# Retention attention and a gelu MLP on one core: quarter-array transposes and values in chunks 1 to 5, masked score blocks left out and k, v loaded with swapped token halves in chunks 2 to 5

## The chip, the cores and the metric

The kernel runs on one core of a Trainium2 chip. The core has TensorE (PE in the profile; its weight loads are PEld), VectorE (DVE), ScalarE (ACT), GpSimd (POOL) and SyncE (SP, which here only issues transfers). Each takes its instructions in order from its own queue. The metric is the device time of one execution in microseconds (us); lower is better.

## The reference

A retention recurrence with a decay per head gives `attn_out`; a two-layer MLP with a tanh gelu follows. Batch 4, 8 heads, 768 tokens, head size 64; d_model 512, d_ff 2048.

```python
def _attn_ref(q, k, v):
    gamma = 1.0 - 2.0 ** (-5.0 - np.arange(H, dtype=np.float32))
    scale = 1.0 / np.sqrt(D)
    ...
    for t in range(S):
        state = gamma[None, :, None, None] * state + np.einsum('bhd,bhe->bhde', k[:, :, t], v[:, :, t])
        y[:, :, t] = scale * np.einsum('bhd,bhde->bhe', q[:, :, t], state)
...
def _moe_ref(x, w_in, w_out):
    h = x @ w_in
    ...
    g = 0.5 * h * (1.0 + np.tanh(c * (h + 0.044715 * h * h * h)))
    return (g @ w_out).astype(np.float32)
```

## The kernel before

**Tiling.** The 768 tokens are cut into 6 chunks of 128 (c = 0 to 5). Inside a chunk the recurrence is turned into matrix products: transposes of q and k (`mm_T`, L266), scores of every key token against every query token (`mm_A`, L273), a causal mask with the decay laid over them on the way out of PSUM (`ev_A1`, L328), the part of the output that comes from the state carried over (`mm_yc`, L289), the part from the chunk's own values (`mm_yi`, L306), and the update of the state (`mm_s` and `ev_S2`). The scores' eviction writes f16 tiles `a` that the values step uses as moving operand. The MLP of a chunk then runs as seven products per block, with sums of weights and activations made by DVE and POOL (L432): `m1w_mm` (L530) for the first layer, `m2w_mm` (L542) for the second; chunk 0 and part of chunk 1 run it plainly (L407, L553).

**TensorE's use of its array.** The MLP products and the transposes use all 128 rows and 128 columns. A transpose by `mm_T` takes a pair of heads, 128x128, so a batch has 8 of them (q and k, 4 pairs each), or 4 in chunks 3 to 5 (`BLK`), where q is transposed by DVE (`trq`, L689). Scores and `mm_yc` use quarters, 64 rows by 64 columns; four of them (two heads j, two halves m of the key tokens) follow one another into the four quarters. A score quarter has 128 columns, all query tokens of the chunk, also where the block of 64 queries by 64 keys lies wholly above the diagonal. `mm_yi` and `mm_s` use all 128 rows and 64 columns.

**Evictions.** `evT` and `evTk` copy transposes from PSUM to SBUF in one instruction per batch (1024 columns, or 512 in chunks 3 to 5); `evA` is one DVE instruction of 512 columns per batch and head parity j; `evY` one per batch.

**Loads.** `load_in` (L765) issues one transfer of 256 KB per input, chunk and batch on SP's queue, all 8 heads, tokens on the partitions. `q_load` (L704) issues 16 of 64 KB for a chunk of `BLK`. `load_dec` (L697) brings a table for `ev_Y1`. Loads and stores keep one order on SP. The weights are triggered from POOL (`trig`, L751), and `hold` (L755) keeps the loads of chunk 1 behind the last trigger and a gelu of chunk 0.

**Order.** Every step is registered as an item with the engines that may run it, and the list `ORDER` (L16) names all items in one sequence, with the letter of the engine for each: p TensorE, a ACT, v DVE, g POOL, s SP (w stands for spin matmuls). Each engine runs its own items in that order and waits in line for what an item needs. PSUM banks (8) and SBUF slots are given out in the same sequence.

## Time and profile before

| | us |
|---|---|
| median of 3 runs | 203.11 (201.61 to 208.5) |
| profiled execution | 201.71 |
| its span, first to last instruction | 199.9 |
| attention steps on PE, busy time over all chunks: L269 128x128 transposes / L278 scores / L309 values / L297 from the state | 10.1 + 1.3 / 7.4 + 0.8 / 6.9 + 1.3 / 3.7 |
| MLP steps on PE, busy time, L542 / L530 / L407 | 69.1 / 63.0 / 31.6 |
| DVE: L329 score evictions, 44 of 512 columns | 27.3 (682 ns each) |
| DVE / ACT: L219 / L217 copies of transposes, 1024 columns | 679 ns / 1017 ns |
| DVE / ACT: the same, 512 columns | 410 ns / 584 ns |
| DVE: L432 `o` with 512 columns / with 256 | 682 ns / 420 ns |
| ACT: one-column activation, L184 | 203 ns |

The page lists, for an engine and a line, how many instructions there are and their busy time; the timeline lists runs of like instructions with their start and length in us. Matmuls overlap, so the length of a run on PE reaches past the start of the next run; what it occupied is the distance between the two starts. The granted TensorE clock is 1.00 in every stage.

### The profile page before, as it was taken

How to read it: one execution, taken by the hardware profiler on the slowest of the kernel's cores; microseconds unless marked ns; L12 is line 12 of the kernel's file. 1: busy time of each engine (PE TensorE's matmuls, PEld its weight loads, DVE VectorE, ACT ScalarE, POOL GpSimd, SP SyncE). 2: the span in 40 equal slices, each digit the busy share in tenths (PEclk: the TensorE clock that was granted, in tenths of full speed). 3: DMA queues.
4: the chain of work that ended last, by engine and by line, in shares of the span. 5: the costliest groups of instructions: out<-in, count | busy, mean ns of one | idle time of the engine just before them, and what ended most of it. 6: DMA issues, size and time to landing. Idle time of an engine off the chain costs nothing.

```text
span 199.9 us, 5916 instructions
## 1 busy us (share of the span) xinstructions
PE 192.4 (96%) x2460; PEld 157.5 (79%) x2460; DVE 151.7 (76%) x278; ACT 123.0 (62%) x233; POOL 108.7 (54%) x109
## 2 busy tenths in 40 slices
PE   7999999989999999999999999999999999999993
PEld 2447895555889898789888899888988888888882
DVE  4366008599788999999999898899697879948730
ACT  2466474023578609999863889857779636786411
POOL 0657000021218575997899579898704967269500
PEclk9999999999999999999999999999999999999999
DMA  6999999998999779987996797610000500002204
GB/s 159 284 267 207 207 204 196 219 258 184 230 241 252 135 132 242 268 130 130 274 257 122 123 223 190 192 48 0 3 0 0 213 3 0 3 0 107 108 26 184
DMA packets 95898, 30.11 MB, mean 151 GB/s; under 512 B 88320, under 2 KB 92800, under 8 KB 95872
## 3 DMA queue, kind: packets, MB, share of 16 engines
q1 hardware_dynamic: 85120, 23.45, 50.6%
q0 software_dynamic: 4224, 4.19, 12.6%
q10 hardware_dynamic: 6528, 2.10, 4.2%
q8 instruction: 19, 0.31, 0.6%
q14 instruction: 7, 0.06, 0.1%
HBM read 27.64 MB, written 6.29 MB: 170 GB/s over the span
## 4 chain that ended last, share of the span: by engine, by line
PE 61%; DMA 14%; DVE 9%; SPq 7%; ACT 3%; POOL 2%; issue 1%; DVEq 0%; ACTq 0%
PE ps L542 26%; PE ps L530 20%; DMA w_out<-in_moe_w_out_dram 10%; PE ps L407 5%; SPq L713 4%; DMA ld<-in_v_dram 3%; SPq L164 3%; PE ps L269 2%; PE ps L278 2%; PE ps L309 2%; PE ps L553 2%; ACT qk L217 2%; DMA ldq<-in_q_dram 1%; DVE s_g L432 1%; DVE st L432 1%
## 5 line engine op out<-in xcount | busy, mean ns | idle before, releaser
L423 ACT ACTIVATE g<-ps 128x512 f16<-128x512 f32 (+1 forms) x56 | 28.3, 538 | 20.6 <-PE ps L407 16.8
L432 DVE TENSOR_TENSOR st<-ps,st 128x512 f32<-128x512 f32 x48 | 31.4, 680 | 5.9 <-PE ps L530 3.0
L542 PEld LDWEIGHTS <-s_g 128*128 128x128 f16 x320 | 31.1, 98 | 4.0 <-DVE s_g L432 0.4
L432 POOL TENSOR_TENSOR s_g<-g 128x512 f16<-128x512 f16 x21 | 24.7, 1184 | 16.9 <-ACT g L423 9.4
L423 ACT ACTIVATE g<-st 128x512 f16<-128x512 f32 x48 | 28.6, 629 | 8.2 <-DVE st L432 7.9
L217 ACT COPY st<-ps 128x512 f32<-128x512 f32 x48 | 26.5, 593 | 8.9 <-PE ps L530 8.8
L407 PE MATMUL ps<-x,w_in 128*128 128x256 f16 (+1 forms) x320 | 30.3, 251 | 0.1
L329 DVE TENSOR_TENSOR a<-ps,mask 128x512 f16<-128x512 f32 x44 | 27.3, 682 | 3.6 <-PE ps L278 3.5
L407 PEld LDWEIGHTS <-w_in 128*128 128x128 f16 x320 | 25.6, 98 | 3.4 <-DMA w_in<-in_moe_w_in_dram 0.3
L530 PEld LDWEIGHTS <-w_in 128*128 128x128 f16 x256 | 24.8, 98 | 3.3 <-issue 0.4
L542 PEld LDWEIGHTS <-g 128*128 128x128 f16 x240 | 22.9, 98 | 3.2
L217 ACT COPY o<-ps 128x512 f32<-128x512 f32 (+1 forms) x28 | 14.5, 528 | 13.8 <-PE ps L542 9.5
L530 PEld LDWEIGHTS <-u_w 128*128 128x128 f16 x192 | 18.5, 98 | 3.2 <-ACT st L217 0.7
L542 PE MATMUL ps<-w_out,s_g 128*128 128x256 f16 x160 | 19.9, 273 | 0.1
L542 PE MATMUL ps<-t_w,s_g 128*128 128x256 f16 x160 | 19.6, 273 | 0.0
L542 PE MATMUL ps<-w_out,g 128*128 128x256 f16 x160 | 19.5, 273 | 0.0
L530 PE MATMUL ps<-xs,u_w 128*128 128x256 f16 x128 | 17.8, 272 | 0.7 <-ACT st L217 0.4
L432 POOL TENSOR_TENSOR s_g<-s_g,g 128x512 f16<-128x512 f16 x14 | 16.3, 1169 | 3.8 <-DVE s_g L432 3.2
L530 PE MATMUL ps<-xs,w_in 128*128 128x256 f16 x128 | 18.4, 273 | 0.0
L432 POOL TENSOR_TENSOR s_g<-g,s_g 128x512 f16<-128x512 f16 x15 | 17.4, 1169 | 1.0 <-DVE s_g L432 0.8
L530 PE MATMUL ps<-x,w_in 128*128 128x256 f16 x128 | 17.4, 273 | 0.2 <-DVE st L432 0.2
L432 DVE TENSOR_TENSOR s_g<-g 128x512 f16<-128x512 f16 x19 | 15.2, 815 | 2.4 <-ACT g L423 2.1
(68 smaller groups left out, 289.7 us busy)
## 6 DMA issues: line engine op xcount, KB each, us to landing
ld<-in_v_dram SPq DMA_DIRECT2D x19, 256.0 KB, 4.3
ld<-in_k_dram SPq DMA_DIRECT2D x17, 256.0 KB, 4.4
out_dram<-o SPq DMA_DIRECT2D x8, 512.0 KB, 3.2
ldq<-in_q_dram SPq DMA_DIRECT2D x48, 64.0 KB, 2.7
w_in<-in_moe_w_in_dram POOLq DMA_DIRECT2D x4, 512.0 KB, 10.3
w_out<-in_moe_w_out_dram POOLq DMA_DIRECT2D x4, 512.0 KB, 15.1
ld<-in_q_dram SPq DMA_DIRECT2D x5, 256.0 KB, 4.5
out_dram<-o SPq DMA_DIRECT2D x5, 256.0 KB, 3.8
```

The costliest lines, as they stand in the source:

```text
L164: eng.dma_start(out=raw[nm, c, b], in_=srcs[nm][b, :, c * C:(c + 1) * C, :].rearrange("h p d -> p h d"),)
L217: eng.copy(out=out, in_=in_)
L269: nc.tensor.transpose(out=ps[:, i, hp], in_=pair(h16[nm, c, b], hp), identity=iden)
L278: nc.tensor.matmul(out=ps[j][m * 64:(m + 1) * 64, hp], lhsT=t[j * 64:(j + 1) * 64, 1, hp, m * 64:(m + 1) * 64], rhs=t[j * 64:(j + 1) * 64, ...
L309: nc.tensor.matmul(out=ps[j * 64:(j + 1) * 64, hp], lhsT=h16["v", c, b][:, 2 * hp + j], rhs=a_sb[c, b, j][:, hp], start=(c == 0), stop=Tru ...
L329: eng.tensor_tensor(out=a_sb[c, b, j], in0=ps, in1=mask[:, j], op=ALU.mult)
L407: nc.tensor.matmul(out=out, lhsT=w_in_sb[wi][:, kc, wr * 128:(wr + 1) * 128], rhs=xT[c][:, kc, t0:t1], start=(kc == 0), stop=(kc == NHP - ...
L423: nc.scalar.activation(out=out, in_=in_, func=AF.Gelu_apprx_tanh, scale=1.0)
L432: eng.tensor_tensor(out=out, in0=in0, in1=in1, op=op)
L530: nc.tensor.matmul(out=ps[:, f], lhsT=m1_lhs(lk, kc, 2 * g + f), rhs=x[:, kc], start=(n in FIRST and kc == 0 and f == 0), stop=(n in (1, 5 ...
L542: nc.tensor.matmul(out=ps, lhsT=m2_lhs(c, lk, fp, a), rhs=m2_rhs(rk, fp), start=(first and fp == 0), stop=(n in (1, 5, 6) and fp == NP - 1 ...
L713: eng.dma_start(out=t[p0:p0 + 32, :, a, :], in_=src[j, dd, t0:t0 + 32])
```

## The change

- Chunks 1 to 5: transposes are made by `mm_T2`, 64x64 at a time, four quarters of the array in turn, and land in two PSUM banks, one for each half m of the tokens. Two copies of half the size (`evTk`, `evTh`) bring them to SBUF.
- Chunks 2 to 5 (`SW` = 2): k and v of heads 4 to 7 are loaded with the two halves of the chunk's tokens swapped on the partitions. `load_in` issues three transfers for it: heads 0 to 3 whole (128 KB), and 64 KB for each half of heads 4 to 7. The new table `cs2` (106 KB, loaded with `dec`) holds k's decay for the swapped order and what the new mask is made of.
- Chunks 2 to 5: scores leave out the block of late keys against early queries, which the mask zeroed. Per pair of heads, one half of the partitions has 128 columns and the other 64; `halves` gives which. `evA2` evicts 384 columns instead of 512. The mask for it is written by two instructions (`scam`) over the old one, after chunk 1's score evictions.
- Chunks 1 to 5: values are made by `mm_yi2` for a pair of batches in two turns of 16 quarter products; in each turn the two row halves write different batches. Between the turns stands `peek`, a copy of one element that needs the first turn's result, and the second turn needs `peek`.
- `ORDER` is new throughout. TensorE's quarter work of chunk 3 reads before: T b2, T b1, T b0, T b3 (in four places); A b2, b3, b0; A b1, yc, yc, S, yi b2, b0, b3, S, yi b1. After (a semicolon stands for MLP work in between): T b0, b1; T b2, b3; A b1, b2, b0; A b3, yc, yc, first turn (0,1); second turn (0,1), first turn (2,3), S, S, second turn (2,3).

The diff, with the lists of `ORDER` left out:

```diff
--- before.py
+++ after.py
@@ -14,58 +14,60 @@
 ORDER = """
...
 """
@@ -102,6 +104,16 @@
     gst_o = np.where(p_i[:, None] < 64, g128[None, 1::2], g128[None, 0::2])
+    late = (p_i[:, None] + 64.0) % 128.0
+    vdec = np.concatenate([kdec[:, :4], gam[None, 4:] ** (160.0 - late)], axis=1)
+    hp_long = np.where(p_i < 64, 0, 2)[:, None, None] + np.arange(2)[None, None, :]
+    ig = np.stack(
+        [1.0 / g128[2 * hp + np.arange(2)[None, :, None]] for hp in (hp_long, (hp_long + 2) % 4)],
+        axis=-1,
+    ).reshape(128, 8)
+    sees = (p_i[:, None] % 64 <= p_i[None, :]).astype(np.float64)
+    cs2_np = np.concatenate([vdec, ig, sees, sees[:, :64]], axis=1).astype(np.float32)
+    cs2_h = nc.inline_tensor(cs2_np, name="rr_cs2")
@@ -120,6 +132,7 @@
     cst = const.tile([128, 192], F32)
+    cs2 = const.tile([128, 16 + 192], F32)
@@ -142,6 +155,7 @@
     BLK = (3, 4, 5)
+    SW = 2
@@ -230,11 +244,11 @@
         else:
-            col = OQ if nm == "q" else OK
+            tab = cst[:, OQ:OQ + H] if nm == "q" else (cs2 if c >= SW else cst[:, OK:])[:, 0:H]
...
                 in0=heads(src, sw),
-                in1=heads(cst[:, col:col + H].unsqueeze(2), sw).broadcast_to(
+                in1=heads(tab.unsqueeze(2), sw).broadcast_to(
@@ -270,15 +284,38 @@
 
+    def mm_T2(c, b, ps, nms):
+        for i, nm in enumerate(nms):
+            for hp in range(NHP):
+                for m in range(2):
+                    rows = slice(m * 64, (m + 1) * 64)
+                    for j in range(2):
+                        nc.tensor.transpose(
+                            out=ps[m][j * 64:(j + 1) * 64, i, hp],
+                            in_=h16[nm, c, b][rows, 2 * hp + j],
+                            identity=iden[rows, rows],
+                        )
...
+    def halves(c, hp):
...
+        if c < SW:
+            return (0, 0, slice(0, 128), hp), (1, 64, slice(64, 128), hp)
+        far = hp > 1
+        return (far, 0, slice(0, 128), hp % 2), (1 - far, 64, slice(128, 192), hp % 2)
...
+    HPS = (0, 2, 1, 3)
...
         t = qkT[c, b]
-        for hp in range(NHP):
-            for m in range(2):
+        for hp in HPS:
+            for m, t0, cols, x in halves(c, hp):
+                if c < SW:
+                    t0, cols = 0, slice(0, 128)
...
                     nc.tensor.matmul(
-                        out=ps[j][m * 64:(m + 1) * 64, hp],
+                        out=ps[j][m * 64:(m + 1) * 64, x, cols],
                         lhsT=t[j * 64:(j + 1) * 64, 1, hp, m * 64:(m + 1) * 64],
-                        rhs=t[j * 64:(j + 1) * 64, 0, hp],
+                        rhs=t[j * 64:(j + 1) * 64, 0, hp, t0:],
@@ -325,8 +362,37 @@
 
+    def mm_yi2(c, bs, ps, turn):
+        for hp in HPS if turn == 0 else HPS[::-1]:
+            for m, t0, cols, x in halves(c, hp):
+                for j in (0, 1) if turn == 0 else (1, 0):
+                    b = bs[m ^ j ^ turn]
+                    nc.tensor.matmul(
+                        out=ps[b][j * 64:(j + 1) * 64, hp, t0:],
+                        lhsT=h16["v", c, b][m * 64:(m + 1) * 64, 2 * hp + j],
+                        rhs=a_sb[c, b, j][m * 64:(m + 1) * 64, x, cols],
+                        start=False,
+                        stop=(turn == 1),
+                        skip_group_check=True,
+                    )
...
+    mask2 = mask.rearrange("p j hp t -> p (j hp t)")[:, 0:768].rearrange(
+        "p (j x t) -> p j x t", j=2, x=2
+    )
...
+    def new_mask(eng, n):
+        lo, hi = ((0, 128), (128, 192))[n]
+        shape = [128, 2, 2, hi - lo]
+        eng.tensor_tensor(
+            out=mask2[:, :, :, lo:hi],
+            in0=cs2[:, 16 + lo:16 + hi].unsqueeze(1).unsqueeze(1).broadcast_to(shape),
+            in1=cs2[:, 8 + n:16:2].rearrange("p (j x) -> p j x", j=2).unsqueeze(3).broadcast_to(shape),
+            op=ALU.mult,
+        )
...
     def ev_A1(eng, c, b, j, ps):
-        eng.tensor_tensor(out=a_sb[c, b, j], in0=ps, in1=mask[:, j], op=ALU.mult)
+        m = mask2 if c >= SW else mask
+        eng.tensor_tensor(out=a_sb[c, b, j], in0=ps, in1=m[:, j], op=ALU.mult)
@@ -603,7 +669,10 @@
         add="v",
+        peek="va",
         evA="v",
+        evA2="v",
+        scam="vg",
@@ -617,6 +686,7 @@
         evTk="va",
+        evTh="va",
@@ -626,6 +696,7 @@
         sume="gv",
+        load3="s",
@@ -697,6 +768,7 @@
             eng.dma_start(out=dec.rearrange("p h t -> p (h t)"), in_=dec_h.ap())
+            eng.dma_start(out=cs2, in_=cs2_h.ap())
@@ -766,13 +838,28 @@
 
+        swap = c >= SW and nm != "q"
...
         def emit(eng):
-            eng.dma_start(
-                out=T[ldk], in_=srcs[nm][b, :, c * C:(c + 1) * C, :].rearrange("h p d -> p h d")
-            )
+            if not swap:
+                eng.dma_start(
+                    out=T[ldk], in_=srcs[nm][b, :, c * C:(c + 1) * C, :].rearrange("h p d -> p h d")
+                )
+                return
+            lo, hi, t0 = slice(0, 64), slice(64, 128), c * C
+            for rows, hs, at in (
+                (slice(0, 128), slice(0, 4), t0),
+                (lo, slice(4, 8), t0 + 64),
+                (hi, slice(4, 8), t0),
+            ):
+                n = rows.stop - rows.start
+                eng.dma_start(
+                    out=T[ldk][rows, hs],
+                    in_=srcs[nm][b, hs, at:at + n, :].rearrange("h p d -> p h d"),
+                )
...
         shape = (SIZE["ld"][1],) if ldk[0] == "st" else ()
-        op("load", emit, [prev[0]], [key], alloc=[(ldk, 1, *shape)],
+        op("load3" if swap else "load", emit, [prev[0]], [key], alloc=[(ldk, 1, *shape)],
@@ -788,22 +875,36 @@
 
+        def T2(b):
+            nms = "k" if c in BLK else "qk"
...
+            def emit():
+                mm_T2(c, b, [T["bank", "T", c, b, m] for m in range(2)], nms)
...
+            for m in range(2):
+                def ev(eng, m=m):
+                    qkT[c, b] = T["qkT", c, b]
+                    copy_on(
+                        eng,
+                        qkT[c, b][:, 2 - len(nms):, :, m * 64:(m + 1) * 64],
+                        T["bank", "T", c, b, m],
+                    )
...
+                new = c not in BLK and m == 0
+                op("evTk" if len(nms) > 1 else "evTh", ev,
+                   [("T", c, b)] + ([] if new else [("al", "qkT", c, b)]), [("kT", c, b, m)],
+                   alloc=[(("qkT", c, b), 1)] if new else [],
+                   early=[("al", "qkT", c, b)] if new else [], free=[("bank", "T", c, b, m)])
+            pe(0.235 if len(nms) > 1 else 0.13, emit, [(nm + "16", c, b) for nm in nms],
+               [("T", c, b)],
+               [(("bank", "T", c, b, m), 1, (128, len(nms), NHP, 64), F16) for m in range(2)],
+               [("qk16", c, b)])
...
         def T1(b):
+            if c:
+                return T2(b)
...
-            if c in BLK:
-                def emit():
-                    mm_T(c, b, T["bank", "T", c, b], "k")
...
-                def ev(eng):
-                    copy_on(eng, T["qkT", c, b][:, 1], T["bank", "T", c, b][:, 0])
...
-                op("evTk", ev, [("T", c, b), ("al", "qkT", c, b)], [("kT", c, b)],
-                   free=[("bank", "T", c, b)])
-                return pe(0.24, emit, [("k16", c, b)], [("T", c, b)],
-                            [(("bank", "T", c, b), 1, (128, 1, NHP, 128), F16)],
-                            [("qk16", c, b)])
@@ -826,11 +927,16 @@
 
-                op("evA", ev, [("A", c, b)], [("a", c, b, j)], alloc=[(("a", c, b, j), 1)],
+                new = c >= SW
+                shape = ((128, 2, 192),) if new else ()
+                op("evA2" if new else "evA", ev, [("A", c, b)] + (["mask0", "mask1"] if new else []), [("a", c, b, j)],
+                   alloc=[(("a", c, b, j), 1, *shape)],
                    free=[("bank", "A", c, b, r)])
-            got = [("qT", c, b), ("kT", c, b)] if c in BLK else [("qkT", c, b)]
+            got = [("kT", c, b, m) for m in range(2)] if c else [("qkT", c, b)]
+            if c in BLK:
+                got.append(("qT", c, b))
             pe(cost, emit, got, [("A", c, b)],
-                       [(("bank", "A", c, b, j), 1) for j in range(2)], [] if c else [("qkT", c, b)])
+                       [(("bank", "A", c, b, j), 1, *(((128, 2, 192),) if c >= SW else ())) for j in range(2)], [] if c else [("qkT", c, b)])
@@ -853,8 +959,26 @@
                early=[] if has_x else [("al", "x", c)], free=[("bank", "Y", c, b)])
+            if c:
+                return
...
+        def yi2(bs):
+            def emit(turn):
+                mm_yi2(c, bs, {b: T["bank", "Y", c, b] for b in bs}, turn)
...
+            def peek(eng):
+                b = bs[halves(c, HPS[-1])[1][0] ^ 1]
+                copy_on(eng, misc[64:65, 1:2], T["bank", "Y", c, b][64:65, HPS[-1], C - 1:C])
...
+            a_of = [("a", c, b, j) for b in bs for j in range(2)]
+            did = ("Yh", c, bs[0])
+            pe(0.182, lambda: emit(0), a_of + [("v16", c, b) for b in bs]
+                       + [("Yc", c, b) for b in bs], [did])
+            op("peek", peek, [did], [("peek", c, bs[0])])
+            pe(0.182, lambda: emit(1), [("peek", c, bs[0])], [("Y", c, b) for b in bs], [],
+                       a_of + [("v16", c, b) for b in bs])
@@ -882,6 +1006,8 @@
                 S1(b)
+        for bs in ((0, 1), (2, 3)) if c else ():
+            yi2(bs)
@@ -1213,6 +1339,10 @@
 
+    for n in range(2):
+        op("scam", lambda eng, n=n: new_mask(eng, n),
+           ["dec"] + [("a", SW - 1, b, j) for b in range(B) if SW > 1 or b > 1 for j in range(2)],
+           [f"mask{n}"])
...
     for c in range(1, NCk):
```

## The prediction

> **What bounds the kernel now.** I read the page's engine table first, then its 40 slices, then the table by stage, the chain of waits, and the timeline of single engines where TensorE changes its work.
>
> ```profile
> PE 192.4 (96%) x2460; PEld 157.5 (79%) x2460; DVE 151.7 (76%) x278; ACT 123.0 (62%) x233; POOL 108.7 (54%) x109
> PE   7999999989999999999999999999999999999993
> DMA  6999999998999779987996797610000500002204
> ```
>
> TensorE (PE) is the only engine that is busy from the second slice to the last but one; the transfers are dense for two thirds of the span and nearly gone after that. The chain of waits ends in 12.24 us of L542 matmuls with nothing between them, and from 84.7 us on it is mostly PE, with DVE in between at 104 to 110. The table by stage shows where PE waits: between 35 and 185 us it stands idle 1.8 us in all. A microsecond of PE work is therefore nearly a microsecond of time, and the question is how much PE work the change removes. The matmul durations of about 220 to 270 ns in the groups are latencies that overlap, so I price by start to start in the timeline of PE:
>
> ```profile
> 49.25 0.61 PE L269 MATMUL ps<-iden,qk 128*128 128x128 f16 x8
> 49.69 2.78 PE L407 MATMUL ps<-x,w_in 128*128 128x256 f16 x24
> ...
> 96.81 0.86 PE L278 MATMUL ps<-qkT 64*64 64x128 f16 x48
> 97.61 1.05 PE L542 MATMUL ps<-t_w,g 128*128 128x256 f16 x8
> ...
> 100.77 0.42 PE L278 MATMUL ps<-qkT 64*64 64x128 f16 x16
> 101.02 0.62 PE L297 MATMUL ps<-qkT,st 64*64 64x128 f16 x32
> ...
> 101.84 0.84 PE L309 MATMUL ps<-a,v 128*64 128x128 f16 x24
> 102.51 0.42 PE L320 MATMUL ps<-v,qk 128*64 128x64 f16 x16
> 102.76 0.39 PE L309 MATMUL ps<-a,v 128*64 128x128 f16 x8
> ...
> 125.76 0.82 PE L542 MATMUL ps<-t_w,g 128*128 128x256 f16 x6
> 126.51 0.64 PE L278 MATMUL ps<-qkT 64*64 64x128 f16 x32
> 127.08 1.05 PE L530 MATMUL ps<-xs,w_in 128*128 128x256 f16 x8
> ```
>
> Read the first column as start, and the next row's start as the time that the work really took. Eight full transposes take 0.44 us: 56 ns each. L278 takes 0.57 us for 32 and 0.80 for 48, so 16 cost 0.225 (four quarters of the array at once, 56 ns a set) and leaving the mode costs 0.10 to 0.12. Six L542 at 109 ns from 125.76 should end at 126.41; L278 starts at 126.51: entering costs 0.10 as well. L309 takes 0.67 for 24: 28 ns each, two column halves at once. L320, 64 columns wide, takes 0.25 for 16: a pair in 32 ns.
>
> **The change on PE.** Pieces are counted in the order list, where every PE step stands in its place.
>
> Transposes of chunks 1 to 5 become sets of four 64x64 quarters, 64 columns each. No row shows this. Nearest below is L320: the whole array is loaded and 64 columns are streamed in 32 ns, though in two pieces, not four. Nearest above is L278: four quarters, 128 columns, 56 ns. I take 32, since the set's columns are those of L320 and L278's four pieces start within 10 ns of each other. A q-and-k step (8 of them) goes from 8 x 56 = 0.448 to 8 x 32 = 0.256, a k step (12) from 0.224 to 0.128: 1.54 + 1.15 = 2.69 us less. At 56 ns it would be nothing.
>
> Scores of chunks 2 to 5 (16 steps of four sets): each column half gets 128, 64, 128, 64 columns and the halves are out of step. If they run freely a set averages (56 + 32) / 2 = 44, which gives 16 x 4 x 12 ns = 0.77 us less; if a set waits for its longest piece, nothing. I take 44: the pieces of a set are started in order, and the next set's wide piece goes to the half that is free first.
>
> Values: a pair of batches goes from 16 matmuls of 28 ns (0.448) to 8 sets; in chunk 1 these are 8 x 56 = 0.448, no gain; in chunks 2 to 5, 8 x 44 = 0.352, 8 pairs, 0.77 less (again nothing if locked).
>
> Against that stand the mode changes. Transposes used to run in the full-array mode of L407, L530 and L542, free of any change (the L269 rows above run on without a gap). Now they are quarter work, and each value step is split in two turns with other work between. In the order list from chunk 0's rest to the end PE changes its mode 43 times before and 71 times after. At 0.097 us (mean of the entries and exits of the timeline, 0.09 to 0.10 each) 28 more cost 2.72 us. The Trainium skill, page "TensorEngine Tiling (Array Packing)", section "Key Properties", says that a change of mode drains the array; the trace agrees, with that 0.10 us.
>
> Sum on PE: -2.69 - 0.77 - 0.77 + 2.72 = -1.5 us. Ends: 0.0 with locked halves, +2.7 if quarter transposes gain nothing either.
>
> **The other engines.** Score evictions of chunks 2 to 5 (32) shrink from 512 to 384 columns: 682 ns at 512 (L329) and 420 at 256 (L432 o), so about 550: 4.2 us less DVE. The order list spends it: 40 half copies of the transposes where 20 whole ones were (DVE 679 ns at 1024 columns, 410 at 512, so about 275 at 256; ACT 1017, 584, about 370), 9.3 us on ACT and 7.8 on DVE (with chunk 0's) against 7 on each; 5 more g sums on DVE at 0.82 instead of POOL at 1.18; 4 state copies from ACT to DVE; two mask products, one on DVE and one on POOL, about 0.4 to 1.2 each, before chunk 2's scores. By these rows each engine's total moves by less than 1.5 us, and none becomes the bound. So I leave the 1.8 us of PE idle as it is; between -1.8 and +3, since every engine's order is new, and an in-order wait can appear anywhere.
>
> Loads: 32 loads of k and v become three issues each, and the table cs2 is one more: 65 issues on SP at 0.37 (shortest L770) to 0.49 (L713), 24 to 32 us. SP waits 59 us for L563 stores, nearly all after 128 us, which doesn't help chunk 2. There SP took 16.2 us (45.4 to 61.6) for 12 loads and dec; at 4 x 0.8 + 24 x 0.43 + 1.3 the new list is 14.8 us: the issues fit into time that the transfers need anyhow. Bytes and 256-byte pieces stay the same. Queued behind is the q load of chunk 3 (L713 at 63.9), for which ACT waits 5.6 us until 75.24. If the cover fails, each us there may be a us of PE; 0 to +2, I take 0.
>
> Peeks (10): the second turn waits on PE for a copy that waits for the first turn; behind it on PE stand all m1 and m2 matmuls. A peek needs 0.22 (last matmul) + what is ahead in ACT's or DVE's queue (0.6 to 0.7 for one instruction) + 0.2 (ACT's one-column L184), about 1.1 us. PE work between the turns, added up from the list with the prices above: 1.06, 1.32, 1.09, 0.87, 1.07, 0.69, 1.94, 2.94, 1.81, 1.07. That covers it to within 0.7 us in all; from 0 to the second rival's price, I take 0. The tail after the last matmul is unchanged.
>
> At the start POOL's two casts of chunk 0 now stand ahead of all the weight triggers: the third w_in trigger (11.72 us) moves behind the cast of 14.71, to 15.3. The weights land one behind the other without a pause until 37 us, 0.5 MB in some 2.6 us, so at 15.3 the first two are still on their way and nothing is lost; if that cover fails, w_in 2 comes up to 3.6 us later, and its first user, 6 us behind the first L407 of 17.2, waits up to 2.
>
> **Sum.** The profiled execution took 201.7 us, 199.9 of span and 1.8 around it; the median of the runs shown, 203.11, is 0.7% above, and I work from 201.7. Forecast 201.7 - 1.5 = 200.2. About 2% (197.7 to 205.7) is what a measurement of this kernel can tell from no change.
>
> **Rivals.**
>
> The waits go as well (0.24). PE loses more than the idle column shows: after 43.49, 78.29, 79.13, 85.6, 110 and 132.2 us the next start comes 0.8, 0.4, 0.57, 0.3, 0.37 and 0.4 us late, 2.8 in all, behind DVE copies, an ACT copy held up by the q casts, and DVE evictions. In the new list q of chunk 3 is issued 4 us of PE work earlier and evictions are shorter. Then 201.7 - 1.5 - 2.8 = 197.4. For it: smaller evictions; against it: the new list fills DVE again.
>
> The peek becomes the wait (0.20), the slower side. If two instructions of 0.6 stand ahead of each peek, 1.62 us are needed and the ten covers fall short by 4.2 in all: 204.4. With three, 2.2 us and 8.9: 209.1. I take the middle, 206.8; from 5.5 us of waits on it is slower by over 2%. For it: DVE is 90 to 100% busy from 65 to 110 us and its queue is rarely empty. Against it: seven of ten peeks are on ACT, 62% busy.
>
> The halves run locked (0.07): PE -0.0, 201.7. The change then leaves blocks out and saves no time by it.
>
> Issue bounds the quarters (0.07). If a quarter matmul with its weights costs 14 ns to issue, as L278's mean, and this isn't the array, none of the three gains comes: +2.7, 204.4. Against it: L278's sets come in bursts of 3 ns with a pause, which looks like the array. The Trainium skill, page "TensorE: Matmul & The Clock Gate", section "Wait — 56ns, not 53.3ns?", sets about 25 ns as the least from start to start however few the columns; by that 16 quarter transposes would take 0.40 us and the change would lose heavily. The trace disagrees for packed tiles: 16 of L278 in 0.225 us.
>
> **Chances.** The forecast, 0.42 (199 to 202 by itself). The waits' case is the one below 197.7; with the forecast's lower tail faster is 0.26. The peek's case alone is slower, 0.20. The rest, 0.54, is within. The range runs from the first rival, 197.3, to just past issue-bound, 205.0, and leaves the peek's case out.
>
> **What would show it.** Quarter transposes 16 in 0.13 us from start to start, scores 16 in 0.18 instead of 0.225, 0.10 us at each change of mode, PE rows of about 2900 matmuls with idle near 2 us, and DVE evictions near 550 ns. Sets of 56 ns for the transposes, gaps on PE after the first turn with the peek as releaser, or ACT waiting for ldq beyond 77 us would prove the forecast wrong.

## The result, and the profile after

The changed kernel takes 231.97 us (median of six runs, 228.68 to 235.01), the kernel before 202.78 beside it. Three of the six were slow runs (232.75 us and more), and the ratio, 1.135 with a 95% interval of 1.125 to 1.145, is of fast runs alone, as all ratios below are. So the change costs 27 us, where 200.2 was forecast with a range up to 205.0. The profiled execution took 229.14 us, 227.3 of span.

These are the engine table, three rows of the 40 slices, the chain of waits and one group of the changed kernel's page:

```profile
PE 197.7 (87%) x2956; PEld 156.5 (69%) x2956; DVE 148.0 (65%) x297; ACT 121.9 (54%) x244; POOL 109.9 (48%) x111
...
PE   7677999998999975499895999880899999999993
...
PEclk9999999999999999589997999997699999999999
DMA  8999999998675667666876777546300220000404
...
PE 51%; DMA 18%; SPq 15%; DVE 4%; ACT 4%; POOL 3%; issue 3%; ACTq 0%; POOLq 0%
PE ps L608 18%; PE ps L596 16%; PE ps L473 10%; SPq L785 8%; SPq L856 6%; DMA w_in<-in_moe_w_in_dram 4%; PE ps L619 4%; DMA out_dram<-o 4%; DMA st<-in_k_dram 3%; DMA st<-in_v_dram 2%; POOL s_g L498 2%; DMA ldq<-in_q_dram 2%; ACT o L231 1%; DVE s_g L498 1%; DVE a L395 1%
...
L231 ACT COPY o<-ps 128x512 f32<-128x512 f32 (+1 forms) x28 | 14.4, 525 | 34.2 <-DMA out_dram<-o 20.2
```

PE has 5 us more of busy time than before and 27 us more of span: it stands idle, in slices 1 to 4, 15 to 17, 22 and 28 above all. The granted clock (PEclk) falls only right behind such a pause. The transfers are thinner than before between 57 and 125 us (DMA 5 to 8 tenths, mostly 6 or 7; before, 6 to 9), and SP's queue holds 15% of the chain of waits, more than twice its share before. So the bytes are not the bound; what hands them out is.

PE's own prices are as forecast. From PE's timeline after (start, length, and the next row's start is the time really taken):

```profile
67.38 0.45 PE L293 MATMUL ps<-iden,qk 64*64 64x64 f16 x32
67.65 0.35 PE L315 MATMUL ps<-qkT 64*64 64x128 f16 x16
67.83 0.36 PE L293 MATMUL ps<-iden,qk 64*64 64x64 f16 x22
...
151.85 0.30 PE L293 MATMUL ps<-iden,qk 64*64 64x64 f16 x16
151.98 0.40 PE L334 MATMUL ps<-qkT,st 64*64 64x128 f16 x16
```

L293 (quarter transposes) takes 0.27 us for 32 and 0.13 for 16, 33 ns a set of four; L315 (scores) 0.18 for 16, 45 ns a set.

Where PE stops, three engines have to be read together. The stall of 5.7 us at 88 us, in the timelines of PE, ACT and SP in turn:

```profile
86.83 1.47 PE L596 MATMUL ps<-x,w_in 128*128 128x256 f16 x12
94.02 3.59 PE L596 MATMUL ps<-xs,u_w 128*128 128x256 f16 x16 [5.71 <-ACT st L231]
```

```profile
89.11 1.87 ACT L231 CAST qk<-ldq 64x512 f16<-64x512 f32 x3 [9.14 <-DMA ld<-in_k_dram]
91.00 0.59 ACT L231 COPY o<-ps 128x512 f32<-128x512 f32 x1
91.48 1.88 ACT L231 CAST qk<-ldq 128x512 f16<-128x512 f32 x3
93.38 1.07 ACT L231 COPY st<-ps 128x512 f32<-128x512 f32 x2
```

```profile
74.18 1.02 SPq L629 DMA_DIRECT2D out_dram<-o  x2
75.30 11.24 SPq L785 DMA_DIRECT2D ldq<-in_q_dram  x16
86.63 3.70 SPq L856 DMA_DIRECT2D ld<-in_k_dram  x6
```

PE waits for ACT's copy of a PSUM bank (st, 93.38). ACT had been free for 9 us, but works in order, and at the head of its queue stood casts of q (qk<-ldq) whose data had not landed. ACT's row names a k load as what ended the wait, because that load counts on a semaphore that one of q's transfers used before it; but the k load of 86.63 landed at 89.49, after the cast had begun. Here are the rows of the tile ldq, which holds q, between 70 and 100 us:

```profile
L785 SPq DMA_DIRECT2D ldq<-in_q_dram x16: 312/487/1862, 75.3 to 86.0; - x16
L231 ACT CAST qk<-ldq x6: 616/616/622, 89.1 to 92.7; 64x512 f16<-64x512 f32 x4, 128x512 f16<-128x512 f32 x2
DMA to landing us min/median/max: 2.8/3.2/3.9
```

The last of q's 16 issues, at 86.05, landed at 89.05, and the cast began at 89.11. It was so late because SP only came to the first of them at 75.30 (63.9 before). The stall of 7.4 us at 152 us goes the same way through a store. One timeline of all engines:

```profile
149.48 6.38 SPq L856 DMA_DIRECT2D ld<-in_v_dram  x8
...
155.95 1.06 SPq L629 DMA_DIRECT2D out_dram<-o  x2
...
159.28 0.59 ACT L231 COPY o<-ps 128x512 f32<-128x512 f32 x1 [8.66 <-DMA out_dram<-o]
...
159.92 2.29 PE L608 MATMUL ps<-t_w,s_g 128*128 128x256 f16 x10 [7.37 <-ACT o L231]
```

The store of the one output tile stands behind eight issues of v; ACT may not write the tile again before it is stored, and PE waits for ACT.

A second loss lies at the start: the first product with w_in (L407 before, L473 after) begins at 20.6 us instead of 17.2, before any split load is issued.

### The profile page after: what moved, and what is told of

Read it like the earlier page. It is cut to its first block, busy times and chain, and to the rows that moved or that the text cites. A ratio compares the mean times of both kernels' runs of the same rounds, so it can differ in the third digit from the quotient of the medians.

```text
span 227.3 us, 7030 instructions
## 1 busy us (share of the span) xinstructions
PE 197.7 (87%) x2956; PEld 156.5 (69%) x2956; DVE 148.0 (65%) x297; ACT 121.9 (54%) x244; POOL 109.9 (48%) x111
## 4 chain that ended last, share of the span: by engine, by line
PE 51%; DMA 18%; SPq 15%; DVE 4%; ACT 4%; POOL 3%; issue 3%; ACTq 0%; POOLq 0%
PE ps L608 18%; PE ps L596 16%; PE ps L473 10%; SPq L785 8%; SPq L856 6%; DMA w_in<-in_moe_w_in_dram 4%; PE ps L619 4%; DMA out_dram<-o 4%; DMA st<-in_k_dram 3%; DMA st<-in_v_dram 2%; POOL s_g L498 2%; DMA ldq<-in_q_dram 2%; ACT o L231 1%; DVE s_g L498 1%; DVE a L395 1%
## 5 line engine op out<-in xcount | busy, mean ns | idle before, releaser
L608 PEld LDWEIGHTS <-s_g 128*128 128x128 f16 x320 | 32.0, 101 | 15.0 <-issue 9.7
L608 PE MATMUL ps<-t_w,s_g 128*128 128x256 f16 x160 | 21.9, 291 | 9.8 <-ACT o L231 9.8
L473 PE MATMUL ps<-x,w_in 128*128 128x256 f16 (+1 forms) x320 | 29.5, 251 | 0.8 <-DMA w_in<-in_moe_w_in_dram 0.8
L596 PEld LDWEIGHTS <-w_in 128*128 128x128 f16 x256 | 25.2, 100 | 5.3 <-DVE x L402 1.6
L473 PEld LDWEIGHTS <-w_in 128*128 128x128 f16 x320 | 25.6, 98 | 3.7 <-DMA w_in<-in_moe_w_in_dram 1.0
L395 DVE TENSOR_TENSOR a<-ps,mask 128x384 f16<-128x384 f32 (+1 forms) x44 | 23.9, 585 | 2.8 <-PE ps L315 2.5
L596 PEld LDWEIGHTS <-u_w 128*128 128x128 f16 x192 | 19.4, 102 | 9.0 <-ACT st L231 6.0
L596 PE MATMUL ps<-xs,u_w 128*128 128x256 f16 x128 | 19.4, 291 | 5.7 <-ACT st L231 5.7
L248 POOL TENSOR_TENSOR v<-ld,cs 128x512 f16<-128x512 f32 x14 | 15.1, 1083 | 16.0 <-DMA ld<-in_v_dram 16.0
L498 DVE TENSOR_TENSOR o<-ps,o 128x512 f32<-128x512 f32 (+1 forms) x18 | 10.6, 595 | 18.7 <-ACT o L231 11.4
L596 PE MATMUL ps<-x,w_in 128*128 128x256 f16 x128 | 18.1, 280 | 1.3 <-DVE x L402 1.3
L596 PE MATMUL ps<-xs,w_in 128*128 128x256 f16 x128 | 18.8, 275 | 0.0
L233 POOL CAST qk<-ld 128x512 f16<-128x512 f32 x9 | 5.8, 650 | 22.3 <-DMA ld<-in_q_dram 10.2
```

Of the source, the lines that this page charges most:

```text
L233: eng.tensor_copy(out=out, in_=in_)
L248: eng.tensor_tensor(out=o, in0=heads(src, sw), in1=heads(tab.unsqueeze(2), sw).broadcast_to([128, NHP, 2, Dh]), op=ALU.mult,)
L395: eng.tensor_tensor(out=a_sb[c, b, j], in0=ps, in1=m[:, j], op=ALU.mult)
L473: nc.tensor.matmul(out=out, lhsT=w_in_sb[wi][:, kc, wr * 128:(wr + 1) * 128], rhs=xT[c][:, kc, t0:t1], start=(kc == 0), stop=(kc == NHP - ...
L498: eng.tensor_tensor(out=out, in0=in0, in1=in1, op=op)
L596: nc.tensor.matmul(out=ps[:, f], lhsT=m1_lhs(lk, kc, 2 * g + f), rhs=x[:, kc], start=(n in FIRST and kc == 0 and f == 0), stop=(n in (1, 5 ...
```

## The experiments

Theories. **Split**: the 64 additional issues of k and v on SP make its queue the bound. **Start**: something else slows the first 20 us. Rivals: TensorE's new order, peeks and mode changes; POOL's casts ahead of the weight triggers; transfers to 64 partitions being slow in themselves.

### What is left without the split: one_issue, split_before, two_plain, no_swap

In one_issue:

```diff
-            if not swap:
+            if True:
```

In split_before, made from the kernel before:

```diff
+            for rows, hs in (
+                (slice(0, 128), slice(0, 4)),
+                (slice(0, 64), slice(4, 8)),
+                (slice(64, 128), slice(4, 8)),
+            ):
+                eng.dma_start(
+                    out=T[ldk][rows, hs],
+                    in_=srcs[nm][b, hs, t0 + rows.start:t0 + rows.stop, :].rearrange("h p d -> p h d"),
+                )
```

In two_plain:

```diff
+            for hs in (slice(0, 4), slice(4, 8)):
                 eng.dma_start(
-                    out=T[ldk][rows, hs],
-                    in_=srcs[nm][b, hs, at:at + n, :].rearrange("h p d -> p h d"),
+                    out=T[ldk][:, hs],
+                    in_=srcs[nm][b, hs, c * C:(c + 1) * C, :].rearrange("h p d -> p h d"),
                 )
```

In no_swap:

```diff
-    SW = 2
+    SW = 6
...
-        op("scam", lambda eng, n=n: new_mask(eng, n),
+        op("scam", lambda eng: None, [], [])
```

> The changed kernel, but each k and v load of chunks 2 to 5 is one transfer of 256 KB again, without the swap of token halves (heads 4 to 7 then hold their tokens in the plain order, which changes the values computed, not the work). Theory Q (SP's queue: three issues of 0.55 to 0.61 us for a load that took about 0.8 make every later load late, and PE waits for it): the waits go, PE's own sum of -1.5 us stays, 199 to 203 us. Rival O (the new order, the peeks, the second PSUM bank or the start of the kernel make the waits): still above 220 us.

211.74 us (ratio 1.045, 1.040 to 1.051), between the two ranges: part of the loss goes with the split, part stays.

> The kernel before, but each k and v load of chunks 2 to 5 is issued as three transfers of the changed kernel's shapes (heads 0 to 3 whole, heads 4 to 7 in two halves of 64 partitions) that bring the same data to the same places. Theory Q: 32 loads x about 1 us more on SP, with SP working without a pause from 50 us on, 212 to 230 us. Rival O: the order of before has its loads early enough, 201 to 206 us.

221.19 us in one run: the kernel before, with nothing but the split, loses 18 us.

> The changed kernel with two transfers of 128 partitions for a k or v load of chunks 2 to 5 (heads 0 to 3 and heads 4 to 7, tokens in the plain order, so other values). Theory Q, number of issues: 1.1 instead of 1.8 us of SP for a load, about halfway, 202 to 214 us. Rival T (what costs is the transfer of 64 partitions, not the issue): as with one transfer, within 1 us of it.

208.45 us in one run. The number lies in theory Q's range, but single loads took 211.74 us, so by this run a second issue of 128 partitions costs nothing, as rival T has it.

> The changed kernel with SW = 6: no chunk is swapped, k and v come in one transfer, scores are whole again with the old mask and DVE evicts 512 columns; transposes and values stay in quarters, with the values' late half still 64 columns wide. Theory Q: PE has the transposes' -2.7, the mode changes' +2.7 and nothing from scores and values, so 201 to 204 us. Rival O: above 220 us.

209.73 us, 207.93 in the profiled run. Loads are single here and no block is left out of the scores. Quarter transposes, values in quarters and peeks stay, and the values still leave out their block, though the short half now always falls on the same rows of the array (the expectation of no_swap_pad, below, names more than the edit undoes). So the split is the larger part, some 18 us, but 5 to 9 remain in every kernel made from the changed one, 3.4 to 3.7 of them in the start (first product with w_in at 20.6 to 20.9 us in each). In all of them the 256-byte packets of the loads take 24 ns (median) in the first 20 us; in the kernel before and in split_before 18. Table cs2, 832 B per partition, stands between the first tables and every tile that loads fill, and all of those now begin 832 B further on, 64 B more than three times 256 B. (No trace holds the addresses themselves; that the tiles began at multiples of 256 B before is the theory's.)

### The addresses: before_shift, after_pad, no_swap_pad, one_issue_pad, before_shift128

In before_shift, made from the kernel before (192 + 32 in before_shift128):

```diff
-    cst = const.tile([128, 192], F32)
+    cst = const.tile([128, 192 + 208], F32)
```

In the kernels whose names end in pad, made from the changed one, no_swap and one_issue, and in all that follow them:

```diff
-    cs2 = const.tile([128, 16 + 192], F32)
+    cs2 = const.tile([128, 256], F32)
...
-            eng.dma_start(out=cs2, in_=cs2_h.ap())
+            eng.dma_start(out=cs2[:, :208], in_=cs2_h.ap())
```

> The kernel before, with 832 B more per partition in its first table (208 columns of cst that nobody reads): every tile behind it, the ones that loads fill among them, moves by the same 832 B as in the changed kernel, and begins 64 B past a multiple of 512 B instead of at a multiple of 256 B. No instruction is added or moved. Address theory: the 256-byte packets of the input loads take 24 to 25 ns in the first 20 us instead of 18, the first matmul with w_in (L407 here) starts 3 us later, at about 20.3 us, and the time is 206 to 210 us. Rival, the order at the start (POOL's casts ahead of the weight triggers): packets at 18 ns, first matmul of the weights at 17.2 us, 203 us.

208.56 us, ratio 1.027 (1.019 to 1.036). Not an instruction differs from the kernel before; the tiles' places alone cost 2.7%.

> The kernel before with its first table 128 B wider per partition (32 columns that nobody reads): every tile behind it begins 128 B past a multiple of 256 B; no other change. If a packet of 256 B only has to begin at a multiple of 128 B: packets 18 ns, 203 us. If it has to begin at a multiple of 256 B: packets 24 to 25 ns in the first 20 us and 206 to 209 us, as with the shift of 64 B.

207.62 us, ratio 1.021 (1.015 to 1.028): a shift by 128 B costs as much. Tables by stage, columns from and to, length, busy time of PE, PEld, DVE, ACT, POOL, clock, share of the DMA engines and GB/s; the kernel before, then before_shift128:

```profile
5.00:10.00 5.00, 4.54 (x44) 2.25 (x43) 1.74 (x3) 2.01 (x3) 3.03 (x4) 1.00 1.26 285
10.00:15.00 5.00, 4.51 (x61) 2.48 (x62) 3.42 (x6) 3.40 (x6) 2.76 (x4) 1.00 1.27 267
```

```profile
5.00:10.00 5.00, 3.34 (x37) 1.67 (x35) 1.00 (x2) 1.53 (x2) 1.75 (x2) 1.00 1.35 218
10.00:15.00 5.00, 4.24 (x56) 2.19 (x54) 2.87 (x5) 2.64 (x5) 4.02 (x5) 1.00 1.35 218
```

The DMA engines are as busy and move 218 GB/s instead of 285; the first L407 starts at 20.67 us, as L473 did in the changed kernel. The Trainium skill, page "DMA: Bandwidth & Descriptors", section "How a descriptor splits into AXI transactions", says that a transaction has to begin at a multiple of 256 B, so that a descriptor which begins elsewhere also carries the bytes from the boundary below it, which nobody uses. It speaks of reads, and here the shifted end is the one that is written; the direction agrees, 18 ns against 24 to 25. By the beats of 32 B that it counts, an estimate, a shift of 128 B should cost more than one of 64 (8 + 4 beats against 8 + 2, for 8 aligned); here the medians of SP's packets in the first 20 us are 25 and 25.

> The changed kernel with its new table padded from 208 to 256 columns (832 to 1024 B per partition), so that the tiles behind it begin at multiples of 256 B again; three issues per load as before. Address theory: packets 18 ns, first matmul of the weights at 17.2 to 17.6 us, and 3 to 6 us less than the changed kernel: 226 us; the queue of the split loads remains with some 20 us. Rival, order at the start: no change, 232 us. Theory that the queue and the packets add up (slower packets make the split loads late too): under 222 us.

226.0 us in two runs, ratio 1.114 (1.101 to 1.126): by the ratios 4.3 us less than the changed kernel. Packets are back at 18 ns, the first L473 at 17.39 us, so the order at the start, POOL's casts first, costs next to nothing. Here is the stage row of after_pad that answers to those above:

```profile
5.00:10.00 5.00, 4.55 (x44) 2.20 (x43) 1.59 (x3) 1.99 (x3) 3.34 (x4) 1.00 1.27 287
```

> The padded table, and no head swapped (SW = 6: single loads, full transposes, full scores and values for all chunks, no second table built): what is left of the change is the order of the work and the table. Address theory: 5 us less than the same without the padding (207.9), so 202 to 204 us, no different from before. Rival, that the new order costs: 206 us or more, with the loss in the start.

205.79 us, ratio 1.007 (1.001 to 1.013): some 4 us of the 209.73 were the addresses, and at most 1.3% is left for the new order, the quarters and the peeks.

> The padded table, single loads of k and v in chunks 2 to 5, unswapped (so heads 4 to 7 are computed with their tokens in plain order: another result), and all of the change on TensorE and on the engines that evict: quarters of transposes, blocks of scores, pairs of values, peeks. Prediction's sum without a cost for loads: 1.5 to 3 us under no_swap_pad, 200 to 202 us. Address theory alone: 211.7 less 5, 207 us, with stalls of 3 to 4 us near 86 us left. Rival, that the peeks and the mode changes take back what the blocks save: the same as no_swap_pad.

202.99 us, ratio 0.9995 (0.995 to 1.004), 9.3 us under one_issue by the ratios. With the table padded, all of the change but the split is worth nothing and costs nothing, to within 0.4%. Against no_swap_pad, whose scores are whole, the ratios differ by 0.8%, 1.5 us, which is the two terms of 0.77 that the prediction had for scores and values, and a set of scores starts every 45 ns here and every 55 there; but with 0.6 and 0.4% to either side the difference in time may be anything from nothing to twice that.

By the ratios (1.135, 1.114, 0.9995) the 27 us are thus 4 of addresses and 23 of split loads. The shares depend on what is taken away first: by one_issue (1.045) they are 18 of split loads and 9 of addresses. The shifted tiles cost the kernel with single loads 9.3 us (1.4 to either side) and the one with split loads 4.3 (3.2 to either side).

### How the split costs: small_halves, hi_act, cast_swap, stores_pool

In small_halves:

```diff
-                (slice(0, 128), slice(0, 4), t0),
-                (lo, slice(4, 8), t0 + 64),
-                (hi, slice(4, 8), t0),
+                (slice(0, 128), slice(0, 7), t0),
+                (lo, slice(7, 8), t0 + 64),
+                (hi, slice(7, 8), t0),
```

In hi_act:

```diff
-                eng.dma_start(
+                (nc.scalar if rows == hi else eng).dma_start(
```

In cast_swap, made from one_issue_pad:

```diff
+        parts = [(slice(0, 128), slice(0, 128), slice(0, NHP))]
+        if c >= SW and nm != "q":
+            lo, hi, near, far = slice(0, 64), slice(64, 128), slice(0, 2), slice(2, 4)
+            parts = [(slice(0, 128), slice(0, 128), near), (lo, hi, far), (hi, lo, far)]
+        for to, at, hps in parts:
+            if tab is None:
+                copy_on(eng, o[to, hps], x[at, hps])
+                continue
             eng.tensor_tensor(
...
+                out=o[to, hps], in0=x[at, hps],
```

In stores_pool:

```diff
-        o.emit(by[e])
+        o.emit(PO if o.kind == "store" and any(x.kind == "load3" for x in items.values()) else by[e])
```

> The padded change with the same three transfers per load on SP, to the same partitions, but heads 0 to 6 in the first and head 7 alone in the two halves (so only head 7 has its tokens swapped; heads 4 to 6 are computed with their tokens in plain order, another result). The bytes through the 64-partition transfers fall to a quarter. Issue theory: an issue costs nearly the same whatever it moves, some 0.4 to 0.6 us each, so most of the 23 us stay: 219 to 226 us. Rival, the bytes that go through 64-partition transfers: about 6 us of the 23, so 209 us.

225.36 us (ratio 1.106): with a quarter of the bytes in the halves, the time is that of after_pad. What costs is the issue, not the bytes that it moves. SP's timelines, first after, then before, in the list of chunk 2:

```profile
59.79 0.61 SPq L856 DMA_DIRECT2D ld<-in_k_dram  x1
60.49 0.55 SPq L845 DMA_DIRECT2D ld<-in_q_dram  x1
61.15 1.85 SPq L856 DMA_DIRECT2D ld<-in_k_dram  x3
```

```profile
49.37 0.74 SPq L770 DMA_DIRECT2D ldq<-in_q_dram  x1
50.20 0.80 SPq L770 DMA_DIRECT2D ldq<-in_k_dram  x1
51.10 1.09 SPq L770 DMA_DIRECT2D ld<-in_q_dram  x1
```

A split load takes SP 1.85 us, three issues without a gap: 0.53 to 0.55 us for four heads of 128 partitions, 0.60 to 0.61 for four heads of 64; a whole q load of 256 KB took 0.55 in the same list (60.49). Summed over the 32 loads of k and v in chunks 2 to 5, SP's issues take 26.9 us in the kernel before, 39.4 in two_plain, whose second issue cost no time, and 63.9 in the changed kernel.

No run issues three transfers of 128 partitions, so the third issue and the 64 partitions aren't told apart. What the page of the changed kernel shows is that a transfer to 64 partitions lands no later than one to 128 (last column, us):

```profile
ld<-in_v_dram SPq DMA_DIRECT2D x16, 128.0 KB, 2.7
ld<-in_v_dram SPq DMA_DIRECT2D x32, 64.0 KB, 2.6
ld<-in_k_dram SPq DMA_DIRECT2D x14, 128.0 KB, 3.4
ld<-in_k_dram SPq DMA_DIRECT2D x28, 64.0 KB, 2.6
```

Between 45 and 158 us SP's issues add up to 100.4 us (159 issues) in after_pad and 70.5 us (96) in one_issue_pad; in the kernel before the last load is issued at 125.6, 81 us after 45. The queue has no room for 100 us in that, and the delay grows from chunk to chunk (start of q's issues, and the last k or v issue, us):

| | q of chunk 3 | q of chunk 4 | q of chunk 5 | last k or v |
|---|---|---|---|---|
| before | 63.9 | 82.1 | 105.2 | 125.6 |
| one_issue_pad | 65.3 | 86.9 | 110.3 | 135.9 |
| after_pad | 72.3 | 99.6 | 128.6 | 156.3 |

The 10 us by which one_issue_pad's last load is late cost nothing; the 31 of after_pad do.

> The padded change with the third transfer of each split load (partitions 64 to 127 of heads 4 to 7) issued by ACT instead of SP; the same bytes in the same shapes. SP then has about 0.54 + 0.61 us for each of the 32 loads instead of 0.54 + 2 x 0.61, 20 us less in all, and ACT 32 x 0.6 = 19 us more between 45 and 135 us, where it was busy 60 to 70% of the time without them. Theory that the issues on SP are the cost (after_pad 226, single loads 203): 207 to 214 us, with the long stalls of TensorE from 85 us on gone or halved. Rival, that transfers to 64 partitions are slow themselves, whoever issues them: 224 to 228 us. Rival, that ACT's evictions queue behind its issues and their waits for free buffers: little gain, 218 us or more, with TensorE waiting for ACT.

237.91 us, ratio 1.163: by the ratios 10 us worse than after_pad, a miss for the theory and the case of the last rival. ACT's and PE's rows of its timeline of all engines:

```profile
53.12 8.43 ACTq L856 DMA_DIRECT2D ld<-in_v_dram  x4
...
61.59 0.62 ACT L231 CAST v<-st 128x512 f16<-128x512 f32 x1 [9.95 <-DMA cs<-rr_cs]
62.24 0.58 ACT L231 CAST x<-ps 128x512 f16<-128x512 f32 x1
62.72 0.59 ACT L231 COPY qkT<-ps 128x512 f16<-128x512 f16 x1
...
63.36 0.64 PE L315 MATMUL ps<-qkT 64*64 64x128 f16 x16 [8.23 <-ACT qkT L231]
```

Four issues of 0.6 us hold ACT for 8.4 us: an issue also waits until its target buffer is free (the third, at 60.18, for a cast by POOL that ended at 60.15), and PE's next eviction (qkT) stands behind it. On SP such a wait delays loads; on an engine that serves PE it stops PE. The Trainium skill, page "Perfetto Trace Analysis", section "DMA Optimizations", says that balancing transfers over the engines that can issue them may help where an engine is busy with issuing. In this case it didn't, on an engine whose other work PE waits for: 237.9 against 226.0 us.

> The padded change with single loads, unswapped, and the swap made when k and v are cast to 16 bits in chunks 2 to 5: one instruction for heads 0 to 3 and two for heads 4 to 7, each from one half of the partitions to the other, in place of one for all; all of the change on TensorE and at the evictions stays. 32 casts become 96 instructions on POOL, ACT and DVE. From q's cast, which goes across partitions in the same way, an instruction more costs its engine some 0.3 to 0.6 us, so 10 to 20 us on each of POOL and ACT. If their idle time covers that, as one_issue_pad: 203 us. Rival, that casts then come late for TensorE: 205 to 210 us. The issue theory needs this to be far under after_pad's 226 us either way.

211.96 us, ratio 1.032 (1.028 to 1.035): by the ratios 17 us under after_pad with the same result, 6.5 over one_issue_pad. POOL's groups of cast_swap, then of one_issue_pad (busy time, mean ns of one):

```profile
L257 POOL TENSOR_TENSOR v<-ld,cst 64x256 f16<-64x256 f32 x28 | 18.0, 642 | 1.9
...
L257 POOL TENSOR_TENSOR v<-ld,cst 128x256 f16<-128x256 f32 x14 | 9.2, 655 | 0.7 <-DMA ld<-in_v_dram 0.2
```

```profile
L248 POOL TENSOR_TENSOR v<-ld,cs 128x512 f16<-128x512 f32 x14 | 15.4, 1111 | 2.1 <-DMA ld<-in_v_dram 2.1
```

Half the partitions cost POOL as much as all (642 against 655 ns), so v's casts go from 15.4 to 27.2 us. Counted by the ratio from one_issue_pad's 203 us that is 209.5, in the range of the rival of late casts; PE's waits, 2.3 us for POOL's xs as the longest, are for POOL, DVE and ACT.

> The padded change with the stores of o that stand among the loads (up to the last split load) issued by POOL instead of SP, at the same place in the order; loads as in the change. Theory that the stores behind the loads are the way (ACT waited 20 us for them, TensorE's stall of 6 us at 151 us and part of the others hang on it): ACT's wait for out_dram falls under 6 us and the time by 6 to 12 us, to 214 to 220 us. Rival, that the loads themselves come late: ACT's waits move to loads, and the time stays at 223 us or more. What POOL adds, six issues of 0.8 us and its waits for o, is under 5 us of an engine that is half idle.

222.69 us, ratio 1.098 (1.088 to 1.107), 3.3 us under after_pad, between the ranges of theory and rival. ACT's wait for out_dram falls from 20.0 us to 6.3; PE's pauses of over 0.1 us still add up to 14.0 us (22.1 in after_pad). By the time, the stores are the smaller way, and most of the loss is in the loads themselves being late.

### The quarters of the transposes: full_T

```diff
-                for m in range(2):
-                    rows = slice(m * 64, (m + 1) * 64)
-                    for j in range(2):
-                        nc.tensor.transpose(
-                            out=ps[m][j * 64:(j + 1) * 64, i, hp],
-                            in_=h16[nm, c, b][rows, 2 * hp + j],
-                            identity=iden[rows, rows],
-                        )
+                m, x = (i, hp) if len(nms) > 1 else (hp // 2, hp % 2)
+                nc.tensor.transpose(
+                    out=ps[m][:, x], in_=pair(h16[nm, c, b], hp), identity=iden
+                )
```

> one_issue_pad with one part of the change on TensorE undone: the transposes of chunks 1 to 5 go over the full array again (112 of 128x128 in place of 448 quarters), into the same two banks, evicted in two halves as in the change. By the prediction's term the quarters save 24 ns a set, so this is 2.7 us slower than one_issue_pad, give or take 1 us for changes of mode: 205 to 206.5 us. Rival, that transposes lie where TensorE waits anyway: no difference, 203 us.

202.72 us, ratio 0.996 (0.993 to 0.999): not slower than one_issue_pad, the time of the rival's case. The profiled one_issue_pad has 4.8 us of pauses of over 0.1 us between matmuls, full_T 1.6. Without them PE takes 193.2 us from its first matmul to the end of its last in full_T, and 192.6 in one_issue_pad (192.5 before). So by one profile of each the quarters save 0.6 us of PE's time, not 2.7; but the recorded ends of the matmuls, some 0.2 to 0.27 us behind their starts, hide shorter pauses. The largest pause of one_issue_pad, 2.2 us before 84.83, has again ACT waiting for q of chunk 3 (until 79.92, in full_T until 74.91); SP begins q's issues at 65.30 there and at 62.94 in full_T. Why, in the same order of work, wasn't settled.

No kernel that computes what the reference asks was clearly under the kernel before.

## Why the prediction was wrong

**The loads failed.** The step said: "the issues fit into time that the transfers need anyhow", and took 0, at most 2 us. Three things were off. The size: 24 issues at 0.43 us came out at 0.53 to 0.61, because rows of other shapes were used as the price (16 by 32 partitions, 0.49, and the shortest issue of all), and chunk 2's list took 24.6 us (49.6 to 74.2), not 14.8. At the prices measured (0.55 for q, 1.77 for the three issues of a load, 1.0 for the tables) it is 17.4; the rest is waits and gaps between the issues. The cover: transfers were no cover, since they thinned out (0.82 of the DMA engines between 40 and 60 us in after_pad, 1.00 before) and landed in some 3 us where the whole loads took 4.4. And the sum was made for chunk 2 alone, with SP's 59 us of waiting for stores, after 128 us, rightly set aside; chunks 3 to 5 have the same list each, no pause between them, and the delay is carried on: +8, +18, +23, +31 us by the table.

**The addresses were not in the sum at all.** The table was counted as one more issue. What it moved, every tile behind it, was no term: 4 us in the changed kernel, 9 with single loads.

**Mechanisms that held.** Quarter transposes 33 ns a set (32 forecast), scores 45 and values 41 to 46 (44), mode changes 79 after against 51 before, the 28 more that were counted; score evictions of 384 columns 548 ns (32 of L395), 550 forecast. The weights at the start came in time once the addresses were right. No peek held PE in the changed kernel or in one_issue_pad by more than a few tenths (once by 1.7 us in after_pad), so the rival on the slower side had the right side and the wrong mechanism. The -1.5 us on PE as a whole did not show: PE's time without pauses is 192.6 us in one_issue_pad and 192.5 before (one profile each, counted as for full_T), and its ratio, 0.9995 with 0.9 us to either side, leaves no such gain in the time. Where it went stays open.

**The test named in the prediction** did show it: "ACT waiting for ldq beyond 77 us" was to prove the forecast wrong, and ACT's first cast of ldq runs at 89.11. The sign doesn't tell how much: in one_issue_pad ACT waits for ldq until 79.92, and the time is that of the kernel before.

## What to carry to other kernels

Price an issue by its own shape, add up all issues of the queue for the whole stretch in which it has no pause, and compare with that stretch: a queue that has to be through with its loads in 81 us has room for 71 us of issues and not for 100, however idle the DMA engines are. Before issues or casts go to another engine, ask what waits there and who stands behind it. After adding a table, think of the tiles behind it, and round its size up to a multiple of 256 B per partition.

## What the runs showed that was not expected

- Moving the tiles that loads fill by 64 or 128 B more than a multiple of 256 B raises the median 256-byte packet of a load from 18 to 24 or 25 ns in the first 20 us, where the DMA share is 1.3; between 40 and 60 us the median is 18 again and the mean 21.7 (before_shift) against 18.0. A spare 192 B per partition is worth 4 us in the changed kernel and 9 in one_issue.
- An issue to 64 partitions takes SP longer (0.60 to 0.61 us) than one of twice the bytes to 128 (0.53 to 0.55).
- Behind PE's pauses of 2.4 to 7.4 us in the changed kernel the granted clock falls: it is 0.53 from 94 to 98 us, 0.62 from 122 to 126 and 0.67 from 160 to 164, and 1.00 in the 4 us behind each. Sixteen matmuls of L596 take 3.39 us from 94.02, at 109 ns each they would take 1.74, so a stall costs more than its length. Behind the pause of 2.2 us in one_issue_pad the clock stays at 1.00.
